# Another written-out order for a state-space layer and an MLP on one core: copies on other engines, other PSUM banks, no fillers

## The chip, the core and the metric

The kernel runs on one core of one Trainium2 chip. The metric is the device time of one execution in microseconds. The kernel before took 228.49, 229.55 and 230.34 us in three runs; the median is 229.55 us. The profile was taken in an execution of its own, in which the span from the first to the last instruction was 226.4 us. What lies outside the span (the start and end of the program) is in the time and not in the profile; the median stands 3.15 us above the span.

Engines are named as the profile names them. PE is TensorE, which multiplies matrices and writes into PSUM; DVE is VectorE; ACT is ScalarE; POOL is GpSimd; SP is SyncE, which here only issues DMAs. Each engine works through its own queue strictly in order; engines wait for each other by semaphores.

## The reference

The input is 2048 positions of 512 channels in bf16. The first half is a layer norm, followed by a convolution along the positions with a kernel made from 128 complex states per channel, and the second half is a layer norm (in effect two, merged) followed by an MLP of width 1376 with a tanh GELU:

```
x = A_u
n = layernorm(x)
K[d,l] = Re( sum_n C[d,n] * exp(dt*A[d,n] * l) * dt*B[d,n] )     # 512 x 2048, 128 states
y = irfft( rfft(n padded) * rfft(K padded) )[:2048] + n * Dskip
h = x + y
z = layernorm(layernorm(h))
out = h + ( gelu(z @ w1 + b1) @ w2 + b2 )
```

## The kernel before

The work is cut along the channels into four chunks of 128 (CW, NCH) and along the positions into two batches of 1024. The kernel K is built from tables of powers: magnitudes by exponentials on ScalarE (L793, 16 of them; L991, 10 of them) and phases by sines. A chain of products on VectorE (L1036 and L1043 in `chain`, L1068 in `chain1`) multiplies magnitudes by the sines that ScalarE makes (L1026 and L1063) from phases that TensorE accumulates (L1013, L1018, L1058, L1061). The products give the pairs of tables EA, EB, IA, IB, and TensorE multiplies them into K (`kgen`, L1092).

For `chain1` the phases must be laid out anew. They are computed on VectorE in `phase` (an arctangent on ScalarE, L883, then a run of six VectorE operations that ends in `split`, L760 to L762), written to DRAM as `HL_d` (L889) and read back (L892). The arctangent needs a product on VectorE (L877) and the table of ScalarE's functions that holds it; the eight sines of the first `chain` are queued behind it on ScalarE.

K then goes through transforms that are matrix products too (`kspec`, `kspec1`, `ktail`, `klate`, `fstage`), partly by a trip through DRAM that changes the layout. The normalised input is transformed in `austage` (L946) and `xspec` (L967, and L971 on VectorE for the second batch). In `inverse` VectorE multiplies spectra (L1235, or L1210 with sums in L1225 for the last chunk of the second batch), TensorE transforms back (L1245), a copy brings the result to SBUF, and a DMA transpose (L1261) turns it. `tail` adds the residual (L1315, L1319, L1322), makes statistics (L1323) and the second layer norm (L1334, L1336). `mlp` does the first product (L1362), the GELU on ScalarE (L1364), the second product (L1378), the sum with the residual on VectorE (L1380) and the output DMAs. There are four MLP passes of 512 positions. From the second half on, products of the MLP of the first batch are mixed with the inverse transform of the second.

Most products end in a copy from PSUM to SBUF by `evac`, which can run on ScalarE (L616) or VectorE (L618). PSUM has eight banks; an `evac` of 1024 columns frees two of them.

What sets the order of the work is a list written out in the source. The program first records 914 operations with their data dependencies (`add`). `ORDER` (L292 to L330) then lists them: an entry is twice the number of the operation, plus one if the second of its two possible engines is to run it. A negative entry is a filler: four small products of an identity on TensorE into a bank that is free and whose result nobody reads (`fill`, L1449, its products at L1451). `SLOTS` (L331) gives the PSUM bank for each new PSUM tile in the order in which they appear. `run` only reads the two strings, and the operations are emitted in the order of the list, so that the list fixes the order within each engine's queue:

```
            o = ops[k // 2]
            o.e = o.eng[k % 2]
            ...
            for p in o.new:
                p.slot = int(next(given))
```

Two fills of zeros (`gap` at L756, called at L757 and L758 for VectorE) are operations 27 and 28, entries 54 and 56 of the list. The product L877 is operation 93 (entry 186), the arctangent operation 126 (entry 252).

Of the kernel before, what the change touches and what calls it, by code (L numbers as in the profile page):

```python
# [275 lines left out]
class VS(V):  # L276
# [13 lines left out]
LAG = {"PE": 0.12, "ACT": 0.20, "DVE": 0.14, "POOL": 0.15, "SP": 0.15}  # L290
OWN = {"PE": 0.0, "ACT": 0.17, "DVE": 0.11, "POOL": 0.1, "SP": 0.0}
ORDER = [  # L292
# [35 lines left out]
]  # L328
SLOTS = "0124624620462046042642640426420206464620242002606204206242604026462064202064026406246024602406206420642016240364710404160364160743104523712460453347247364163210657000423751452706341725310671620547"


TURN = 450000
# [2 lines left out]
class Sched:  # L335
# [54 lines left out]
    def run(self, nslots):  # L390
# [13 lines left out]
        taken = [None] * nslots  # L404
        given = iter(SLOTS)
        order, seen = [], set()
# [1094 lines left out]
```

## Time and profile before

| | before |
|---|---|
| median time of three runs | 229.55 us (228.49 to 230.34) |
| span of the profiled execution | 226.4 us |
| PE busy | 198.1 us (87%) |
| DVE busy | 174.3 us (77%) |
| ACT busy | 164.9 us (73%) |
| POOL busy | 13.8 us (6%) |
| chain that ended last, by engine | PE 65%, ACT 17%, DVE 11%, DMA 3% |

A row of the chain or the timeline reads: start in us from the span's beginning, duration in us, engine, what is written, line of the kernel, number of instructions. In the timeline, square brackets give the idle time ahead and who ended it. A row of the groups reads: line, engine, operation, what is written from what, partitions x elements and types, number of instructions; then busy us in all and the mean ns of one; then the idle time just before them. In PE rows a tile such as 128\*32 is the part of the array that a product uses (rows \* columns). The slices of the page are 5.66 us each, and a digit is the busy share in tenths. "ps" is PSUM, "ar" the one large SBUF tile.

### The profile page before, as it was taken

To read this page: it belongs to the slowest core of one execution; us is meant where nothing else is said; L and a number is where in the kernel's file an instruction comes from. 1 tells how busy PE (TensorE), PEld (TensorE's weight loads), DVE (VectorE), ACT (ScalarE), POOL (GpSimd) and SP (SyncE) were. 2 spreads that over 40 slices of the span, in tenths; PEclk is the share of its full clock that TensorE was granted. 3 is DMA by queue.
4 is the path that set the end of the run, shared out by engine and by line. 5 is a ranking of instruction groups with operands and counts; after the bars stand their busy time and mean duration, and the time that the engine had idled before them with its cause. 6 is when DMAs were issued, how large, how long until landed. Compare 5 with 4: busy or idle time off the path is not lost.

```text
span 226.4 us, 6876 instructions
## 1 busy us (share of the span) xinstructions
PE 198.1 (87%) x2989; PEld 112.4 (50%) x2989; DVE 174.3 (77%) x277; ACT 164.9 (73%) x205; POOL 13.8 (6%) x26
## 2 busy tenths in 40 slices
PE   6314977768999999999999868999999999999993
PEld 3102743234767478566576556644443444444552
DVE  7999789999998898889999999899827476013022
ACT  4999999999988998989999469695156206801900
POOL 2000301200010003000000010300000101000000
PEclk9999999999999999999999999999999999999998
DMA  5992074250003964657789495383050131313202
GB/s 152 179 189 74 7 243 128 50 146 6 6 3 75 130 174 135 163 143 213 163 176 280 136 306 110 108 191 90 0 127 0 32 88 46 72 44 78 75 23 70
DMA packets 43159, 25.09 MB, mean 111 GB/s; under 512 B 30197, under 2 KB 40697, under 8 KB 43130
## 3 DMA queue, kind: packets, MB, share of 16 engines
q1 hardware_dynamic: 42968, 24.59, 45.2%
q8 instruction: 23, 0.38, 0.7%
q10 hardware_dynamic: 162, 0.07, 0.1%
q14 instruction: 6, 0.05, 0.1%
HBM read 14.13 MB, written 5.28 MB: 86 GB/s over the span
## 4 chain that ended last, share of the span: by engine, by line
PE 65%; ACT 17%; DVE 11%; DMA 3%; issue 2%; POOL 0%; DVEq 0%; ACTq 0%; SPq 0%; POOLq 0%
PE ps L1378 17%; PE ps L1362 17%; PE ps L1092 8%; ACT ar L793 7%; PE ps L1245 6%; PE ps L946 4%; DVE ar L1235 4%; ACT ar L616 4%; PE ps L967 3%; ACT ar L1063 3%; ACT ar L991 3%; DVE ar L618 2%; DMA HL_d<-ar 2%; PE ps L1145 1%; PE ps L1061 1%
## 5 line engine op out<-in xcount | busy, mean ns | idle before, releaser
L616 ACT CAST ar<-ps 128x1024 bf16<-128x1024 f32 (+4 forms) x72 | 61.9, 903 | 14.0 <-PE ps L1245 9.2
L1364 ACT ACTIVATE ar<-ps,ar 128x512 bf16<-128x512 f32 (+1 forms) x44 | 27.0, 692 | 28.7 <-PE ps L1362 20.5
L1378 PE MATMUL ps<-ar 128*128 128x512 bf16 (+3 forms) x187 | 40.2, 367 | 0.0
L1362 PE MATMUL ps<-ar 128*128 128x512 bf16 (+1 forms) x176 | 39.8, 379 | 0.0
L1380 DVE TENSOR_TENSOR ar<-ps,ar 128x512 bf16<-128x512 f32 (+1 forms) x17 | 10.8, 655 | 28.3 <-PE ps L1378 28.3
L1378 PEld LDWEIGHTS <-ar 128*128 128x128 bf16 (+1 forms) x187 | 17.9, 98 | 19.7 <-issue 0.7
L1362 PEld LDWEIGHTS <-ar 128*128 128x128 bf16 (+1 forms) x176 | 17.3, 100 | 20.5 <-issue 0.8
L1235 DVE TENSOR_TENSOR ar<-ar 128x2048 bf16<-128x2048 bf16 x20 | 23.9, 1220 | 1.0 <-PE ps L1245 0.5
L1245 PE MATMUL ps<-ar 64*128 64x128 bf16 x672 | 21.7, 216 | 3.1 <-DVE ar L1235 2.1
L618 DVE CAST ar<-ps 128x1024 bf16<-128x1024 f32 (+3 forms) x19 | 21.3, 1129 | 3.3 <-PE ps L946 1.7
L1245 PEld LDWEIGHTS <-ar 64*128 64x128 bf16 x672 | 19.0, 94 | 7.8 <-DVE ar L1235 4.6
L1063 ACT ACTIVATE ar<-ps 128x1024 bf16<-128x1024 int16 x20 | 19.7, 1027 | 1.7 <-PE ps L1061 1.0
L1092 PE MATMUL ps<-ar 128*52 128x66 bf16 x512 | 19.4, 242 | 0.3 <-DVE ar L618 0.2
L1092 PEld LDWEIGHTS <-ar 128*52 128x52 bf16 x512 | 16.9, 130 | 4.4 <-issue 2.6
L689 POOL TENSOR_TENSOR ar<-ar 128x4 f32<-128x4 f32 (+1 forms) x6 | 8.6, 1436 | 141.7 <-DVE ar L694 99.5
L946 PE MATMUL ps<-ar 128*32 128x512 bf16 x256 | 15.9, 381 | 0.5 <-ACT ar L991 0.3
L793 ACT ACTIVATE ar<-ar 128x1024 bf16<-128x1024 f32 x16 | 15.7, 1045 | 0.6 <-DVE ar L788 0.6
L1026 ACT ACTIVATE ar<-ps 128x1024 bf16<-128x1024 int16 x16 | 15.7, 1033 | 0.3 <-PE ps L1018 0.2
L1068 DVE TENSOR_TENSOR ar<-ar 128x1024 bf16<-128x1024 bf16 x20 | 13.1, 685 | 1.2 <-ACT ar L1063 1.0
L967 PE MATMUL ps<-ar 128*64 128x512 bf16 (+2 forms) x160 | 14.0, 298 | 0.1
L1322 DVE TENSOR_TENSOR ar<-ps,ar 128x512 bf16<-128x512 f32 x12 | 8.0, 683 | 7.9 <-ACT ar L1364 4.3
L1061 PE MATMUL ps<-ar 128*32 128x256 f16 (+1 forms) x256 | 12.7, 301 | 1.2 <-ACT ar L1063 1.1
(85 smaller groups left out, 232.0 us busy)
## 6 DMA issues: line engine op xcount, KB each, us to landing
ar<-in_A_u_dram SPq DMA_DIRECT2D x16, 128.0 KB
ar<-in_A_u_dram SPq DMA_DIRECT2D x8, 256.0 KB
out_dram<-ar SPq DMA_DIRECT2D x30, 64.0 KB
ar<-in_B_w_dram SPq DMA_DIRECT2D x4, 344.0 KB
ar<-in_B_w_dram SPq DMA_DIRECT2D x2, 640.0 KB
AK_d<-ar SPq DMA_DIRECT2D x2, 512.0 KB
ar<-AK_d SPq DMA_DIRECT2D x2, 512.0 KB
AKc_d<-ar SPq DMA_DIRECT2D x4, 256.0 KB
```

What stands on the lines that cost most here:

```text
L616: act.copy(out_fn(), in_fn())
L618: dve.tensor_copy(out_fn(), in_fn())
L793: add("ACT", c_act(1024) + 0.03, lambda e, e0=e0: act.activation(free(EB0 // 2 + 4 * (16 - e0), [[8 * e0, 2], [4 * NB, NCH * CW // 4], [1, ...
L946: pe.matmul(pst(p)[32 * j:32 * j + 32, 512 * z:512 * z + 512], lhsT=BX.ap()[:, f0 + z, 16 - 16 * c:48 - 16 * c], rhs=src[2 * j + c].ap(), ...
L967: pe.matmul(pst(p)[64 * h:64 * h + 64, w * (k + r):w * (k + r) + w], lhsT=T.ap()[:, f, r, :], rhs=v[f:f + 1].ap()[:, 0, :], start=True, st ...
L1063: add("ACT", c_act(1024), lambda e, sc=sc: act.activation(sc.ap().rearrange("p z a b -> p (z a b)").rearrange("p (x a f) -> p a x f", a=4, ...
L1092: pe.matmul(o, lhsT=free(ta.lo // 2 + q * 4 * NP_ + f, [[4, NP_ + NA]]), rhs=free(tb.lo // 2 + q * 4 * NB + f, [[4, 2 * NB]]), start=ta is ...
L1235: dve.tensor_tensor(pq.ap().rearrange("p n d -> p (n d)"), a, b_, ALU.mult)
L1245: pe.matmul(pst(p)[:, 512 * h + 128 * k:512 * h + 128 * k + 128], lhsT=q.ap()[rows, x, :], rhs=TP[w].ap()[rows, f0 // 2 + k, :], start=(n ...
L1362: pe.matmul(pst(p)[:fs], lhsT=w1s[dc].ap()[:, fc * P:fc * P + fs], rhs=ybuf.ap().rearrange("p (t c) k -> p c t k", c=4)[:, dc], start=(dc ...
L1364: add("ACT", c_act(512, 1), lambda e, p=p, fc=fc, fs=fs: act.activation(hT.ap()[:fs, fc, :], pst(p)[:fs], ACT.Gelu_apprx_tanh, bias=b1_sb. ...
L1378: pe.matmul(pst(p)[:, c0:c1], lhsT=hT.ap()[:fs, fc, 128 * t:128 * t + 128], rhs=w2s[fc].ap()[:fs, c0:c1], start=(fc == 0), stop=(fc == NFC ...
```

## The change

`ORDER` and `SLOTS` are replaced. The 914 operations, their data and their dependencies stay the same; what each engine does when, and some choices of engine, are different:

- The two fillers (entries -1 and -5) are gone.
- ScalarE's queue has 198 entries where it had 208, VectorE's 291 where it had 277, SP's 127 where it had 131. TensorE's 278 and POOL's 20 are only reordered. Of the operations that may run on either engine, 23 go from ScalarE to VectorE and 9 from VectorE to ScalarE; four DMA issues go from SP's queue to ScalarE's.
- Up to the last sum of spectra (L1225), VectorE has 20 operations more from ScalarE: ten copies of 1024 float columns (among them the two of 1024 columns at L843 and in the first half of `S3`, L867, and the ones of `austage` and `fstage`), one of 924, one of 264, four of 512, one of 576 on 64 partitions, one bf16 copy of 1024 and one of 512 columns, and one scaling of 512 columns out of PSUM (L1334). It has eight fewer: four copies of 1024, one of 512, a bf16 copy of 1024, and two scalings of 512.
- The two fills of zeros (entries 54 and 56), second and third in VectorE's queue before, stand between the layer norm's statistics and behind its scalings.
- On TensorE products with the same part of the array stand next to each other more often: along its queue the part changes 97 times where it changed 119 times. The products of `tail` for the second batch (L1319) stand in one group of eight.
- Two pieces of the second MLP product (L1378, six matrix products) stand ahead of the last group of L1245, and one piece of the first (L1362, four) behind it, where they stood the other way round.
- SP's queue takes the first loads in another order: slices of the input come ahead of some of the parameters, the order of the two halves of the phase tables is turned, and the constants of W come before those of T.
- PSUM tiles go to other banks.

The diff, cut to the first lines of the two lists, the lines with the entries named above, and the strings of banks:

```diff
 ORDER = [
-    294, 0, 50, 2, 4, 62, 52, 154, 6, 64, 54, 8, 102, 12, 56, 66, 14, 10, 136, 16, 68, 58, 104, 32, 190, 106, 30, 96, 98, 76, 164, 60, 26, 22, 138,
...
-    184, 430, 434, 170, 432, 436, 112, 242, 116, 438, 42, 248, 188, 130, 442, 132, 458, 448, 232, 226, 452, 454, 450, 194, 210, 244, 214, 228, 218,
-    212, 128, 202, 134, 222, 220, 196, 224, 456, 446, 216, 444, 238, 186, 240, 234, 236, 472, 475, 468, 250, 252, 284, 484, 488, 471, 487, 298, 254,
-    256, -1, 490, 302, 258, 260, 262, 300, 312, 264, 306, 304, 204, 316, 460, 314, 320, 318, 326, 328, 330, 266, 340, 310, 332, 462, 476, 342, 334,
-    280, 268, 206, 308, -5, 270, 344, 338, 346, 776, 778, 348, 792, 794, 336, 272, 286, 352, 354, 356, 324, 384, 350, 360, 358, 479, 386, 390, 274,
...
+    0, 6, 2, 4, 8, 52, 64, 50, 102, 194, 62, 12, 10, 66, 68, 154, 96, 84, 26, 86, 16, 104, 58, 72, 76, 14, 136, 106, 22, 98, 108, 78, 202, 60,
+    141, 138, 118, 120, 142, 122, 80, 144, 146, 148, 124, 151, 190, 70, 18, 32, 94, 30, 34, 152, 156, 74, 192, 28, 110, 112, 164, 176, 178, 158,
+    160, 166, 20, 162, 24, 414, 422, 168, 416, 171, 180, 172, 175, 418, 426, 126, 92, 128, 428, 424, 36, 82, 420, 204, 88, 434, 210, 100, 182,
+    430, 284, 212, 432, 226, 436, 206, 228, 242, 438, 208, 44, 40, 54, 116, 440, 218, 442, 446, 244, 458, 114, 456, 222, 454, 450, 452, 220, 448,
+    444, 56, 214, 288, 46, 224, 188, 238, 230, 240, 216, 38, 132, 246, 232, 234, 248, 236, 130, 476, 90, 472, 479, 460, 475, 468, 184, 488, 290,
+    298, 250, 463, 186, 302, 471, 491, 196, 772, 252, 300, 312, 304, 254, 314, 134, 256, 764, 306, 282, 258, 260, 316, 308, 326, 262, 318, 264,
...
 ]
-SLOTS = "0124624620462046042642640426420206464620242002606204206242604026462064202064026406246024602406206420642016240364710404160364160743104523712460453347247364163210657000423751452706341725310671620547"
+SLOTS = "1071346036024602640264024606206462002466242662060260246422064206420642426046024602462046204602462042604236013563701341437047362475270173103564261507610452173052365432601267465024572161254203721432"
```

60 rows, old and new, of the table ORDER are left out of this document.

## The prediction

> **What bounds the kernel now.** I read the page first (busy shares, the 40 slices, the chain), then the chain in order of time, then the busy time by stretch.
>
> ```profile
> span 226.4 us, 6876 instructions
> PE 198.1 (87%) x2989; PEld 112.4 (50%) x2989; DVE 174.3 (77%) x277; ACT 164.9 (73%) x205; POOL 13.8 (6%) x26
> ...
> PE   6314977768999999999999868999999999999993
> ...
> DVE  7999789999998898889999999899827476013022
> ...
> PE 65%; ACT 17%; DVE 11%; DMA 3%; issue 2%; POOL 0%; DVEq 0%; ACTq 0%; SPq 0%; POOLq 0%
> ```
>
> TensorE is the longest row, but from slice 1 to slice 28 (some 160 us) VectorE stands at 8 or 9 nearly throughout; only behind that has it room. So a copy put on VectorE is cheap late and dear early. The chain in order of time:
>
> ```profile
> 36.04 0.70 DVE ar L694
> ...
> 39.89 4.31 DMA HL_d<-ar
> 44.27 2.24 DMA ar<-HL_d
> ...
> 46.55 0.40 PE ps L1058 x4
> 46.95 0.22 PE ps L1061 x8
> ...
> 47.66 1.75 ACT ar L1063 x2
> ...
> 56.89 1.47 PE ps L1092 x40
> ...
> 163.43 0.55 PE ps L1245 x16
> 163.98 1.41 PE ps L1378 x6
> ...
> 222.89 0.04 issue
> ```
>
> A VectorE run ends in the split of the phases (L762), which goes out to DRAM and back (HL_d, 39.89 to 46.51), releases the sines of chain1 (L1063, from 47.66), and these release the first kernel products (L1092, 56.89). From there TensorE leads. The last product of the second inverse (L1245) starts at 163.43 and ends at 163.98; behind it TensorE runs to 222.89 without a wait in the chain, and 3.5 us of output follow. The busy time by stretch, cut where VectorE starts, where the split ends, at the first L1092, at 140.3, and where VectorE has finished the last combination (L1225) that the last L1245 group needs:
>
> ```profile
> core 0: us, PE busy (x) PEld busy (x) DVE busy (x) ACT busy (x) POOL busy (x), PEclk, DMA share, GB/s
> 4.42:39.88 35.46, 20.29 (x348) 12.08 (x345) 32.89 (x63) 34.83 (x40) 2.99 (x4) 1.00 0.61 138
> 39.88:56.89 17.01, 13.25 (x256) 5.69 (x249) 16.68 (x22) 16.40 (x18) 1.47 (x6) 1.00 0.24 67
> 56.89:140.30 83.41, 79.04 (x1909) 54.57 (x1909) 78.13 (x118) 73.58 (x89) 3.91 (x4) 1.00 0.61 146
> 140.30:162.40 22.10, 22.10 (x175) 11.10 (x171) 20.75 (x27) 14.06 (x20) 2.00 (x1) 1.00 0.47 115
> ```
>
> VectorE is busy 32.89 + 16.68 + 78.13 + 20.75 = 148.45 us of these 157.97: it idles 9.5 us (2.57, 0.33, 5.28, 1.35). TensorE idles 4.4 us from 56.89 to 140.3 and none after. Both engines are nearly full here, VectorE 94%.
>
> **The copies, which carry the sum.** Up to that last L1225 the new VectorE queue holds 20 operations that ScalarE had, and gives 8 away (counted by reading both orders). Their durations:
>
> ```profile
> L618 DVE CAST ar<-ps 128x1024 bf16<-128x1024 f32 x14 | 16.9, 1218 | 2.0 <-PE ps L946 1.7 <-PE ps L1120 0.3
> L1036 DVE TENSOR_TENSOR ar<-ar 128x1024 bf16<-128x1024 bf16 x16 | 10.5, 683 | 0.0
> L931 DVE TENSOR_SCALAR ar<-ar 128x512 bf16<-128x512 bf16 x16 | 5.5, 406 | 0.1
> L618 DVE CAST ar<-ps 128x512 bf16<-128x512 f32 x3 | 2.1, 692 | 0.8 <-PE ps L1145 0.6 <-ACT ar L616 0.3
> L618 DVE CAST ar<-ps 128x924 bf16<-128x924 f32 x1 | 1.1, 1120 | 0.5 <-PE ps L1092 0.5
> L618 DVE COPY ar<-ps 128x1024 bf16<-128x1024 bf16 x1 | 0.7, 676 | 0.0
> ```
>
> Added: ten copies of 1024 at 1.218 (12.2), one of 924 (1.1), four of 512 (2.8), one bf16 copy (0.7), and four small ones with no VectorE row of their own (264, 576 and twice 512 columns), between 0.4 and 0.7 each by the L931 and 512 rows, together 1.6 to 2.8; I take 2.2, the middle. Sum 19.0. Given away: four of 1024 (4.9), one of 512 (0.7), the bf16 copy (0.7), two scalings at 0.41 (0.8): 7.1. Net 11.9 us. Back to back they overlap a little:
>
> ```profile
> 1.25 1.34 DVE L756 MEMSET ar<- 128x1536 f32 x1 [0.27 <-issue]
> 2.85 1.34 DVE L756 MEMSET ar<- 128x1536 f32 x1 [0.27 <-issue]
> 4.42 0.69 DVE L689 TENSOR_TENSOR ar<-ps,ar 128x512 f32<-128x512 f32 x1 [0.23 <-ACT ar L701]
> ...
> 31.13 0.68 DVE L689 TENSOR_TENSOR ar<-ar 128x512 f32<-128x512 f32 x1
> 32.53 3.49 DVE L618 CAST ar<-ps 128x1024 bf16<-128x1024 f32 x3 [0.72 <-PE ps L946]
> ...
> 161.72 0.69 DVE L1225 TENSOR_TENSOR ar<-ar 128x512 bf16<-128x512 f32 x1
> ```
>
> Three copies take 3.49, 1.163 each, 0.955 of the mean; so 11.9 becomes 11.4. The two L756 fills of zeros ran before 4.42, while VectorE had nothing else. The change queues them among the statistics of the layer norm, behind real work: 2.6 us more. VectorE's work from 4.42 to the last L1225 becomes 148.45 + 11.4 + 2.6 = 162.45 us. With no idle at all it ends at 166.9; with the old 9.5 us of idle at 176.4; it ended at 162.4.
>
> **Where idle remains.** Through the split L762 the new queue has four more 1024 copies (4.65), two L1036 products (1.3) and the two fills (2.6) ahead of it; of the old idle of 2.57 I let 1.0 stay (the POOL power function is still waited for). The split then ends at 39.87 + 8.55 - 1.57 = 46.9, 7.0 late. The DRAM trip of 6.6 us is unchanged, so L1058 comes at 53.5, the first sine L1063 at 54.7 and L1092 at 63.9. Between 46.9 and the end of the first sine VectorE has eight products of the first chain and one copy queued, and I let it wait 1.0 us. For the rest (old idle 6.96) I take 2.5: more work queues up and ScalarE, lighter by the same copies, delivers earlier. Idle 4.5 in all, last L1225 at 171.4, last L1245 group (0.55, and a release) done at 172.1.
>
> **ScalarE's front.** Two copies of 1024 columns leave it ahead of the table load that the sines need.
>
> ```profile
> L616 ACT CAST ar<-ps 128x1024 bf16<-128x1024 f32 x47 | 46.0, 1022 | 13.1 <-PE ps L1245 9.2 <-PE ps L967 1.2 <-issue 1.1
> ```
>
> ```profile
> 35.37 0.63 ACT L701 ACTIVATE ar<-ar 128x512 f32<-128x512 f32 x1
> 36.80 3.77 ACT L1026 ACTIVATE ar<-ps 128x1024 bf16<-128x1024 int16 x4
> ```
>
> The arctangent (L883) at 35.37 could come 2.0 us earlier, at 33.4, but it waits for the product at L877 (31.13 to 31.81 before). That stands behind five more copies (5.8) and the fills (2.6), less about 1.1 of absorbed idle: done at 39.1. All eight chain sines (L1026) are queued behind the arctangent on ScalarE, so they start near 39.9 in place of 36.80. The relief is worth nothing.
>
> **TensorE.** Shape changes along its queue fall from 119 to 97 (counted on both orders). Their price:
>
> ```profile
> 60.51 0.41 PE L1018 MATMUL ps<-ar 64*32 64x512 f16 x8
> 60.85 0.69 PE L1092 MATMUL ps<-ar 128*52 128x66 bf16 x16
> ```
>
> Eight L1018 products between groups of another shape hold TensorE 0.34 us from start to start; eight L1061 after a group of the same shape take 0.22 (the chain at 46.95; both are one pass of 512 columns' time). An excursion is 0.12, a change 0.06: 22 changes save 1.3 us, of which 10 lie between L1092 and the last L1245 (0.6) and 8 behind it (0.5). The two fillers (four small products each) stand where TensorE waits anyway for ScalarE or for HL_d: nothing. Between the first L1092 and the last L1245 the work is the same but for six L1378 products drawn ahead (1.4, as the chain shows for just these at 163.98) and four L1362 of the same shape put off (0.9). TensorE alone would reach that group's end at 63.9 + 102.7 (79.04 + 22.10, and all of the 1.58 us to 163.98) + 1.4 - 0.9 - 0.6 = 166.5, with the old idle of 4.4 at 170.9. VectorE's 172.1 decides, narrowly. Behind it: 58.9 - 1.4 + 0.9 - 0.5 = 57.9 us to 230.0, plus 3.5: span 233.5. The eight L1319 groups, now in one piece, wait for a ScalarE copy and a DMA transpose behind the last L1245; 24 L1362 products cover these in the new order, where 30 products did before and nothing waited. The six missing bound the loss: 0 to 1.4 us; I take 0.
>
> **Edits at nothing.** Other PSUM banks: a bad choice costs a wait for one copy (1.2); I see none and keep it in the range. Four DMA issues go from SP's to ScalarE's queue, which has become lighter; SP's reordered loads move data that VectorE uses later than before.
>
> The span grows by 7.1 us. The median of 229.55 stands 3.15 us above this profile's span; with the same distance the time is 236.6.
>
> **The rivals.**
>
> *TensorE leads and ScalarE's front shortens (faster).* If the L877 product is there when the table is (33.4), the front is 2.0 us earlier, and the shape changes give 1.3: 226.3 us. For it: TensorE's 65% of the chain, ScalarE's 17%. Against it: VectorE's 9.5 us of idle can't hold 13.9 us of new work. It decides only if VectorE's product at L877 ends by 33.4. 6%.
>
> *The lag is made up (no change).* The split is late, but TensorE's 4.4 us of idle and VectorE's 9.5 go to nearly zero and the six early L1378 products fill in: 229.5 to 231.8. Even zero idle gives 232.1, so it needs copies cheaper than their rows. 12%.
>
> *TensorE at half pace.* A longer wait for HL_d empties TensorE. After the waits early on:
>
> ```profile
> 12.95 0.40 PE L865 MATMUL ps<-ar 128*32 128x256 f16 x1 [5.09 <-DMA ar<-tab_I]
> ...
> 22.57 2.75 PE L988 MATMUL ps<-ar 128*32 128x256 f16 x48 [2.03 <-DVE ar L618]
> 24.66 2.85 PE L988 MATMUL ps<-ar 128*32 128x256 f16 x56
> ```
>
> From 22.57 to 24.66, 40 products, 10 passes of 256 columns four abreast, take 2.09 us, about twice the pace of the L1061 row, though the granted clock reads 1.00 in every stretch above. If L1092 begins so after some 4 us without products, 6 us at half pace lose 3: TensorE's 170.9 becomes 173.9, past VectorE, span 235.3 and 238.4 us; a second such stretch gives 241.4. [...] Against it: the products of chain1 follow the sines, two in 1.75 us at 47.66, which half pace still keeps up with, and VectorE leaves TensorE 1.2 us in hand. 10%.
>
> *VectorE decides, as summed.* 72%, at 236.6.
>
> **How the numbers follow.** VectorE's idle from 0 to 9.5 spans 232.1 to 241.6; leaving out the last microsecond, and taking in the upper half of the no-change case, the range is 230.8 to 240.6. About 6% faster, 6% at the lower no-change end and 7% above are left out. Within 1% (227.3 to 231.8; about what a measurement can tell from no change): 12%. Faster 6%, slower 82%.
>
> **What would show it.** VectorE's slices at 9 through slice 29; TensorE with more idle from 40 to 64 us and again short waits on VectorE before L1245; L883 released by VectorE, not by the table load; HL_d's write starting near 47, the first L1092 near 64, the last L1225 near 171; L1319 in one group. I am wrong if the first L1092 is before 60, or if TensorE runs from it to the last L1245 without waiting on VectorE.

## The result, and the profile after

The changed kernel takes 239.98 us (median of six runs, 239.15 to 240.34) where the kernel before takes 228.95: the ratio is 1.0472, with a 95% interval from 1.0439 to 1.0505. It is slower, and the time lies inside the forecast range (230.8 to 240.6), 3.4 us above the forecast of 236.6 and close to its upper end. The profiled execution took 240.18 us with a span of 238.4 us, so 1.8 us lie outside the span. The forecast had added 3.15 us, the distance of the old median from the old profile's span; that hid a part of the miss, since in spans it is 238.4 against 233.5, 4.9 us.

Line numbers of the changed kernel are one higher than those of the kernel before (L1092 is now L1093, L1245 is L1246, L1225 is L1226). The page of the changed kernel, busy shares, slices and chain:

```profile
span 238.4 us, 6848 instructions
PE 200.7 (84%) x2973; PEld 115.6 (48%) x2981; DVE 184.4 (77%) x291; ACT 156.6 (66%) x191; POOL 14.4 (6%) x26
...
PE   6204958559899989999998885999999999999994
...
DVE  2999999995999899899999898799993748313022
...
PEclk9999988956999999999999997999999999999999
...
PE 47%; DVE 22%; issue 20%; DMA 3%; ACT 2%; POOL 2%; SPq 0%; DVEq 0%; POOLq 0%; ACTq 0%
```

ScalarE has lost 8 us of work (164.9 to 156.6) and VectorE has gained 10 (174.3 to 184.4). VectorE stands at 9 in most slices up to slice 29, TensorE has fallen to 5 in the eighth and ninth slice (42 to 54 us), and its share of the chain went from 65% to 47%, VectorE's from 11% to 22%. Of the 20% called "issue", 42.86 us are one stretch (99.98 to 142.84) in which the chain follows POOL; the timeline says that POOL waits there for VectorE (42.90 us, until L695), so VectorE's share is larger than the 22% show. The chain of the changed kernel in order of time:

```profile
46.78 4.27 DMA HL_d<-ar
...
51.10 2.20 DMA ar<-HL_d
...
53.34 0.62 PE ps L1059 x4
...
65.72 1.96 PE ps L1093 x54
...
142.88 1.93 POOL ar L690
144.83 0.17 DVE ar L695
...
145.86 0.40 PE ps L1347 x4
146.26 3.23 PE ps L1246 x64
...
153.94 1.89 PE ps L1246 x64
...
176.75 0.58 PE ps L1246 x16
177.36 5.34 PE ps L1363 x24
182.70 1.85 PE ps L1320 x16
```

HL_d's write starts at 46.78 in place of 39.89, the first kernel product comes at 65.72 in place of 56.89 (8.8 us late), the last inverse product at 176.75 in place of 163.43 (13.3 late). L1320 (the former L1319) runs in one piece and waits for nothing.

The end of the chain has another shape than the forecast gave it. TensorE's last wait of more than 0.2 us lies at L1347, at 145.86, and is 2.88 us long: VectorE's statistics end near 142.8, then come POOL's power function, VectorE's L695 and ScalarE's L1337. Behind it TensorE runs to 234.84. In the kernel before, its last such wait (0.69 us, for VectorE's L1235) ended at 138.41, and TensorE ran from there to 222.89. So of the span's 12.0 us, 7.45 lie ahead of TensorE's last wait and some 4.5 behind it, where the new list leaves TensorE more to do; 1.3 of these are half pace, 64 products of L1246 that take 3.23 us at 146.26 (granted clock 0.55 from there to 149.5) and 1.89 at 153.94 (1.00).

The busy time by stretch, with the cuts of the forecast: the end of the split, the first L1093, the first L1363, the end of the last L1226:

```profile
core 0: us, PE busy (x) PEld busy (x) DVE busy (x) ACT busy (x) POOL busy (x), PEclk, DMA share, GB/s
4.42:46.76 42.34, 22.80 (x376) 12.46 (x374) 40.65 (x70) 34.78 (x39) 3.18 (x7) 0.96 0.44 112
46.76:65.72 18.96, 13.82 (x212) 5.72 (x211) 16.07 (x21) 13.89 (x16) 1.03 (x3) 0.73 0.24 70
65.72:151.19 85.47, 77.86 (x1842) 55.21 (x1845) 79.33 (x120) 67.35 (x79) 4.97 (x5) 0.98 0.63 150
151.19:176.70 25.51, 25.30 (x240) 13.28 (x241) 24.64 (x32) 15.19 (x22) 1.86 (x1) 1.00 0.31 73
sum 172.28, PE 139.78 PEld 86.67 DVE 160.68 ACT 131.22 POOL 11.04; mean PE 34.94 PEld 21.67 DVE 40.17 ACT 32.80 POOL 2.76
```

Up to the end of the last L1226 VectorE is busy 160.68 of 172.28 us and idles 11.6 (1.69, 2.89, 6.14 and 0.87 by stretch). Before, it was busy 148.46 of 157.99 and idled 9.5. So of the 14.3 us by which this point is later, 12.2 are work and 2.1 are idle. The forecast had counted on more work (162.45) and on far less idle (4.5). Up to the first L1093 the 8.8 us are 7.1 of work and 1.7 of idle, behind it the 5.5 are 5.1 and 0.4. From the end of the last L1226 to the end of the span the changed kernel needs 61.7 us where 64.0 were needed before; the forecast had 62.1.

### The profile page after: what moved, and what is told of

It is laid out like the page before. It is cut to its first block, busy times and chain, and to the rows that moved or that the text cites. A ratio compares the mean times of both kernels' runs of the same rounds, so it can differ in the third digit from the quotient of the medians.

```text
span 238.4 us, 6848 instructions
## 1 busy us (share of the span) xinstructions
PE 200.7 (84%) x2973; PEld 115.6 (48%) x2981; DVE 184.4 (77%) x291; ACT 156.6 (66%) x191; POOL 14.4 (6%) x26
## 4 chain that ended last, share of the span: by engine, by line
PE 47%; DVE 22%; issue 20%; DMA 3%; ACT 2%; POOL 2%; SPq 0%; DVEq 0%; POOLq 0%; ACTq 0%
PE ps L1363 16%; PE ps L1379 16%; DVE ar L619 6%; DVE ar L924 4%; PE ps L1246 3%; PE ps L1093 3%; DVE ar L690 3%; DVE ar L1069 3%; DVE ar L695 2%; POOL ar L690 2%; PE ps L1062 2%; DMA HL_d<-ar 2%; PE ps L947 2%; PE ps L1059 1%; ACT ar L1064 1%
## 5 line engine op out<-in xcount | busy, mean ns | idle before, releaser
L617 ACT CAST ar<-ps 128x1024 bf16<-128x1024 f32 (+4 forms) x60 | 52.4, 920 | 21.5 <-PE ps L1246 6.2
L1365 ACT ACTIVATE ar<-ps,ar 128x512 bf16<-128x512 f32 (+1 forms) x44 | 28.0, 686 | 28.1 <-PE ps L1363 26.2
L1363 PE MATMUL ps<-ar 128*128 128x512 bf16 (+1 forms) x176 | 40.1, 379 | 0.1
L1379 PE MATMUL ps<-ar 128*128 128x512 bf16 (+3 forms) x181 | 38.7, 366 | 0.4 <-issue 0.2
L619 DVE CAST ar<-ps 128x1024 bf16<-128x1024 f32 (+5 forms) x31 | 32.6, 1066 | 2.3 <-PE ps L1146 0.8
L1363 PEld LDWEIGHTS <-ar 128*128 128x128 bf16 (+1 forms) x176 | 17.3, 100 | 20.3 <-issue 0.6
L1246 PE MATMUL ps<-ar 64*128 64x128 bf16 x672 | 22.6, 224 | 0.6 <-DVE ar L1236 0.6
L1064 ACT ACTIVATE ar<-ps 128x1024 bf16<-128x1024 int16 x20 | 19.7, 1032 | 4.2 <-PE ps L1062 3.4
L1246 PEld LDWEIGHTS <-ar 64*128 64x128 bf16 x672 | 20.1, 98 | 4.4 <-issue 1.9
L947 PE MATMUL ps<-ar 128*32 128x512 bf16 x256 | 18.3, 427 | 3.4 <-DVE ar L932 2.6
L1093 PE MATMUL ps<-ar 128*52 128x66 bf16 x512 | 18.3, 243 | 0.6 <-DVE ar L1069 0.6
L1093 PEld LDWEIGHTS <-ar 128*52 128x52 bf16 x512 | 16.7, 129 | 3.1 <-issue 1.7
L968 PE MATMUL ps<-ar 128*64 128x512 bf16 (+2 forms) x160 | 14.4, 304 | 4.1 <-DVE ar L619 1.7
L1062 PE MATMUL ps<-ar 128*32 128x256 f16 (+1 forms) x256 | 13.9, 327 | 1.5 <-ACT ar L1064 1.4
L947 PEld LDWEIGHTS <-ar 128*32 128x32 bf16 x256 | 7.4, 105 | 12.2 <-issue 5.2
```

The lines of the kernel that those rows point to most:

```text
L617: act.copy(out_fn(), in_fn())
L619: dve.tensor_copy(out_fn(), in_fn())
L947: pe.matmul(pst(p)[32 * j:32 * j + 32, 512 * z:512 * z + 512], lhsT=BX.ap()[:, f0 + z, 16 - 16 * c:48 - 16 * c], rhs=src[2 * j + c].ap(), ...
L1064: add("ACT", c_act(1024), lambda e, sc=sc: act.activation(sc.ap().rearrange("p z a b -> p (z a b)").rearrange("p (x a f) -> p a x f", a=4, ...
L1093: pe.matmul(o, lhsT=free(ta.lo // 2 + q * 4 * NP_ + f, [[4, NP_ + NA]]), rhs=free(tb.lo // 2 + q * 4 * NB + f, [[4, 2 * NB]]), start=ta is ...
L1246: pe.matmul(pst(p)[:, 512 * h + 128 * k:512 * h + 128 * k + 128], lhsT=q.ap()[rows, x, :], rhs=TP[w].ap()[rows, f0 // 2 + k, :], start=(n ...
```

## The experiments

### All 32 engine choices, in either order

In the new list the 32 operations that changed between ScalarE and VectorE were given back their old engines (a_engines_before), and in the old list they got the new ones (b_engines_after). Nothing else was edited; an entry's last bit is the engine:

```diff
 ORDER (new list)
-  ..., 141, ..., 171, ..., 463, ..., 491, ...   # operations 70, 85, 231, 245 and 28 more
+  ..., 140, ..., 170, ..., 462, ..., 490, ...
```

> The new order and banks, but all 32 copies and scalings on the engine that the old order gave them. If VectorE's load is the cause: 11.4 us of VectorE work go, VectorE no longer decides the last L1246, and most of the loss returns: 230 to 233 us. If the order and the banks themselves are the cause: 237 us or more, since only engine choices change. If TensorE's half pace is the cause: the wait for HL_d and the slow products behind it stay, so 236 us or more.

> The mirror image: the old order, banks and fillers, with the 32 engine choices of the new one. If VectorE's load is the cause: 11.4 us more on VectorE against 9.5 us of its idle, which can't all be used: 233 to 238 us. If order and banks are the cause: 228 to 231 us.

The new list with the old engines took 249.96 us (1.0892, 1.0839 to 1.0945), 10 us more than with its own engines; the old list with the new engines took 262.81 us (1.1443, 1.138 to 1.1505). The load theory fell in both. The first time lies in the open ranges of the two other theories (237 or more, 236 or more), but in the mirror image the theory of order and banks, with 228 to 231, fell as well. VectorE's work alone does not explain the times: in the first it is busy 150.88 us up to the end of the last L1226, nearly as little as in the kernel before, and idles 30.9. Neither the engines nor the order accounts for the times by itself: what an engine choice is worth depends on the place in the queue. The next two runs show that for three of the 32 operations.

### Two single choices that hold up a queue

```diff
 ORDER (new list, a_first_back)         ORDER (old list, b_two_over)
-  141                                  -  1081   1086
+  140                                  +  1080   1087
```

> The new list with one copy given back to ScalarE, operation 70 (1024 columns, the first table of phases). Theory 'VectorE has no slack, and only the load counts': 1.2 us less, 238.8. Rival 'a copy on the other engine holds up the queue it joins': on ScalarE it stands behind three exponentials at L794 and VectorE's first L848 waits for it, as where all old engines were put into the new order (L848 at 13.27 in place of 9.48, 3.8 us late); with VectorE without slack these 3.8 us go through to the end: 243 to 244.

> The old list with two operations of the second half given to VectorE in their places, as in the new list: 540 (a scaling of 512 columns in the first tail, L1334) and 543 (a copy of 512 columns of the transposed rows). Load theory: 0.4 + 0.7 us more on VectorE, 229.5 to 230.4. Rival 'held up queue': the two stand in VectorE's queue ahead of products of spectra (L1235) that the inverse transform waits for, and they themselves wait for the statistics and the power function on POOL; where all new engines were put into the old order VectorE waited 3.37 and 4.20 us near there: 4 to 7 us, so 233 to 236.

a_first_back took 243.83 us (1.0658, 1.061 to 1.0706), 3.85 us more than the changed kernel, though VectorE has a copy less. Its ScalarE and its VectorE near the place, from the timeline (start, duration, then in brackets the idle time ahead):

```profile
7.52 4.82 ACT L794 ACTIVATE ar<-ar 128x1024 bf16<-128x1024 f32 x5
12.25 0.99 ACT L617 CAST ar<-ps 128x1024 bf16<-128x1024 f32 x1
```

```profile
13.27 1.23 DVE L848 TENSOR_TENSOR ar<-ps,ar 128x1024 f32<-128x1024 f32 x1 [4.72 <-ACT ar L617]
```

The copy stands behind a row of exponentials on ScalarE (the last five are shown), and L848 starts at 13.27 where the changed kernel starts it at 9.48. The 3.8 us arrive undiminished at the end of the last L1226 (180.25 against 176.70, and 3.85 in the time). That is the held-up queue, as expected (243 to 244). The load theory, which gave 238.8, is out for this operation.

b_two_over took 238.19 us (1.0395, 1.0336 to 1.0454): 9.1 us for 1.2 us more of work on VectorE, more than the 4 to 7 expected. VectorE of that kernel, from the timeline:

```profile
138.82 0.80 DVE L1334 TENSOR_SCALAR ar<-ps,ar 128x512 bf16<-128x512 f32 x1
...
145.57 2.36 DVE L1235 TENSOR_TENSOR ar<-ar 128x2048 bf16<-128x2048 bf16 x2 [3.96 <-PE ps L1245]
...
155.80 1.22 DVE L1210 TENSOR_TENSOR ar<-ar 128x1024 f32<-128x1024 bf16 x1 [5.04 <-PE ps L1245]
```

and its TensorE:

```profile
139.68 0.61 PE L1346 MATMUL ps<-ar 128*128 128x128 bf16 x4 [3.11 <-DVE ar L1334]
...
142.36 3.60 PE L1245 MATMUL ps<-ar 64*128 64x128 bf16 x64 [0.33 <-ACT ar L616]
```

The scaling L1334 waits its turn in VectorE's queue; TensorE's L1346 waits 3.11 us for it, L1245 stands behind that in TensorE's queue, and keeps VectorE waiting in turn. What is more than expected is TensorE's pace: the granted clock is 0.88 from 140 to 180 (1.00 in the kernel before), the 64 products at 142.36 take 3.60 us (1.96 at 153.79 in the same run), and 16 products of L1362 at 148.56 take 5.30 (3.63 in the kernel before), together 3.3 us. In both whole lists these bits are set the right way for their own order. That a held-up operation holds all that stands behind it is seen where all old engines stand in the new list, with the same 4.72 us before L848: the fill L1280, which reads nothing, starts there at 19.83 in place of 16.03.

### Six copies that only shift load

Six copies for which the receiving queue has room in both orders: in the new list they go back to ScalarE (a_six_back), in the old list to VectorE (b_six_over).

```diff
 ORDER (new list, a_six_back)           ORDER (old list, b_six_over)
-  171 463 585 731 771 935              -  170 462 584 730 770 934
+  170 462 584 730 770 934              +  171 463 585 731 771 935
```

> The new list, six of the copies that went to VectorE given back to ScalarE in their places (operations 85, 231, 365 and 385 with 1024 columns, 292 with 924, 467 with 512). Theory 'VectorE has no slack in the new order': these six take 4 x 1.22 + 1.12 + 0.69 = 6.7 us on VectorE, and ScalarE idles enough to take them, so the time falls by 5 to 6.7 us, to 233.3 to 235; the split ends near 44.3 (two copies less), the last L1226 near 170. Rival 'the order of the list sets the time, and VectorE's load is not what decides': 239 to 240.5.

> The old list with the same six copies given to VectorE that a_six_back gives back (85, 231, 292, 365, 385, 467). Theory 'VectorE decides in the old order too, though it idles 9.5 us up to the last L1225': 4 to 6.7 us more, 233 to 236. Rival 'TensorE leads in the old order and VectorE's idle takes the copies in': 229 to 230.5.

b_six_over took 234.28 us, 5.2 more than the kernel before (1.0251, 1.0174 to 1.0328: clearly slower, though not clearly by more than 2%) and inside the 4 to 6.7 expected. a_six_back took 237.02 us (1.0345, 1.0288 to 1.0401), 3.0 less than the changed kernel; that is 2 us above the one expectation and 2 us below the other. Its runs scatter from 235.72 to 237.93; the profiled one, with 235.72 the quickest, has a span 4.5 us shorter (233.9 against 238.4), and the profiles are compared here. The busy time from 4.42 to the end of the last combination in each (columns as above), first b_six_over:

```profile
4.42:168.60 164.18, 136.70 (x2671) 85.23 (x2673) 154.40 (x233) 134.34 (x159) 10.38 (x15) 0.98 0.52 126
```

and a_six_back:

```profile
4.42:172.30 167.88, 136.15 (x2670) 86.44 (x2671) 155.11 (x234) 135.69 (x159) 11.05 (x16) 0.96 0.50 124
```

| | VectorE work to the last L1225 | its idle | ends at |
|---|---|---|---|
| before | 148.46 | 9.5 | 162.4 |
| before, six copies on VectorE | 154.40 | 9.8 | 168.6 |
| after, six copies back on ScalarE | 155.11 | 12.8 | 172.3 |
| after | 160.68 | 11.6 | 176.7 |

Two things follow. The six copies, 6.7 us by their rows (four at 1.22, 1.12 and 0.69), change VectorE's work by 5.94 and 5.57 us, 0.89 and 0.83 of the rows. In part that is because an operation starts before the one ahead of it has ended (in the changed kernel a copy of 1.21 us at 22.06 is followed at 23.18); the rest is not explained. And in the old order the 5.94 us of work move the end by 6.2: the 9.5 us of idle took in nothing. In the new order 5.57 us of work move it by 4.4 in the quickest run and the time by 3.0 in the median. Four of the waits show why. VectorE's timeline in the kernel before:

```profile
28.32 0.17 DVE L694 SCALAR_TENSOR_TENSOR ar<-ar 128x8 f32<-128x8 f32 x1 [1.20 <-POOL ar L689]
...
89.40 0.17 DVE L694 SCALAR_TENSOR_TENSOR ar<-ar 128x8 f32<-128x8 f32 x1 [0.54 <-POOL ar L689]
...
123.32 2.36 DVE L1235 TENSOR_TENSOR ar<-ar 128x2048 bf16<-128x2048 bf16 x2 [0.45 <-PE ps L1245]
...
145.66 0.16 DVE L694 SCALAR_TENSOR_TENSOR ar<-ar 128x4 f32<-128x4 f32 x1 [0.90 <-POOL ar L689]
```

and with the six copies added (b_six_over):

```profile
29.42 0.17 DVE L694 SCALAR_TENSOR_TENSOR ar<-ar 128x8 f32<-128x8 f32 x1 [1.20 <-POOL ar L689]
...
92.16 0.17 DVE L694 SCALAR_TENSOR_TENSOR ar<-ar 128x8 f32<-128x8 f32 x1 [0.54 <-POOL ar L689]
...
128.07 2.36 DVE L1235 TENSOR_TENSOR ar<-ar 128x2048 bf16<-128x2048 bf16 x2 [0.45 <-PE ps L1245]
...
151.73 0.16 DVE L694 SCALAR_TENSOR_TENSOR ar<-ar 128x4 f32<-128x4 f32 x1 [0.90 <-POOL ar L689]
```

The same waits, to the hundredth, 1 to 6 us later. They are round trips: VectorE gives work to another engine and then needs its answer. When VectorE comes later, the answer comes as much later. These four are 3.1 of the 9.5 us. Most of the others stay within 0.1 us as well, but not all: two waits for L1063's sines (0.22 and 0.77) are gone, so is one of 0.25, one for L1145 grew from 0.21 to 0.81, and one of 1.23 came before an L1235, while TensorE's granted clock had fallen (0.97 from 140 to 180, 1.00 in the kernel before). That the sum hardly changed is in part chance.

### Front and rest

The first 250 entries of one list (they end about where the first L1092 starts), then the remaining operations in the order of the other; PSUM banks had to be handed out anew, and the fillers are kept only with the old front.

```diff
 ORDER (h_old_front)                    ORDER (h_new_front)
+  entries 1 to 250 of the old list     +  entries 1 to 250 of the new list
+  then the new list without these      +  then the old list without these
```

> The first 250 entries of the old list (they run up to about the first L1092, with their engines, and without four of the 1024 copies on VectorE), then the other operations in the new order with the new engines; PSUM banks handed out anew. Theory 'VectorE's extra work adds up and its waits stay, so a lag is carried through to the end': the new kernel's first L1093 was 8.8 us late, so 7 to 9 us of the 11 go: 231 to 233; first L1093 near 57, last L1226 near 168. Rival 'the lag of the front is made up behind it, where TensorE and VectorE had waits to give': 237 to 240. Rival 'the front is all of it': 228 to 230.

> The mirror of it: the first 250 entries of the new list with their engines, then the other operations in the old order with the old engines; PSUM banks handed out anew, no fillers. Theory 'carried through': 7 to 9 us over the kernel before, 236 to 238. Rival 'made up behind the front': 229 to 232. Sum of this excess and of h_old_front's: about 11 us if the parts add up.

h_old_front took 232.7 us (1.0159, 1.0124 to 1.0193: less than 2%, but clearly slower), where 231 to 233 was expected, h_new_front 238.83 us (1.0439, 1.0389 to 1.0488), somewhat above the 236 to 238 expected: 3.35 and 9.5 us over the kernel before, 12.8 together where the whole change costs 11.0. Nothing was made up behind the front:

| | first L1092 | end of last L1225 | rest of the span |
|---|---|---|---|
| before | 56.9 | 162.4 | 64.0 |
| old front, new rest | 57.5 | 168.6 | 62.4 |
| new front, old rest | 66.5 | 172.4 | 64.8 |
| after | 65.7 | 176.7 | 61.7 |

The new front alone is 9.6 us late at the first kernel product and 10.0 us late at the last combination. The new middle part adds 5.5 us (0.6 to 6.2 late with the old front, 8.8 to 14.3 in the whole change), and the new end gives about 2 us back. So the span's 12.0 us are 8.8 of the front, 5.5 of the middle and 2.3 the other way from the end. Up to the last combination VectorE works 154.11 us and idles 10.1 with the old front, and works 154.99 and idles 13.0 with the new one (148.46 and 9.5 before): again no idle is used up, and the new front adds some.

### The fills of zeros

```diff
 ORDER (new list, a_zeros_first)
-  0, 6, 2, 4, 8, ... 40, 54, 116, ... 444, 56, 214, ...
+  0, 6, 2, 54, 56, 4, 8, ... 40, 116, ... 444, 214, ...
```

> The new kernel with the two fills of zeros back at the head of VectorE's queue, where VectorE has nothing else. VectorE's load: 2.6 us less work, of which up to the old idle may be lost again: 237.3 to 238.5 us, the write of HL_d about 2 us earlier than 46.78. The other theories: no change of more than 0.5 us.

It took 239.77 us (1.0449, 1.04 to 1.0497): no change, where 237.3 to 238.5 was expected from the load. Where the fills stood in the changed kernel, from VectorE's timeline:

```profile
28.93 1.34 DVE L757 MEMSET ar<- 128x1536 f32 x1 [0.27 <-issue]
...
30.50 0.17 DVE L695 SCALAR_TENSOR_TENSOR ar<-ar 128x8 f32<-128x8 f32 x1 [0.21 <-POOL ar L690]
...
33.64 1.34 DVE L757 MEMSET ar<- 128x1536 f32 x1 [0.27 <-issue]
```

and without them (a_zeros_first):

```profile
30.50 0.17 DVE L695 SCALAR_TENSOR_TENSOR ar<-ar 128x8 f32<-128x8 f32 x1 [1.75 <-POOL ar L690]
...
35.45 1.23 DVE L619 CAST ar<-ps 128x1024 bf16<-128x1024 f32 x1 [1.74 <-PE ps L947]
```

L695 starts at 30.50 in both. The fills lay inside two round trips, to POOL's power function and to the product L947; the one place where VectorE's idle is good for something is work put into the wait itself.

### Fillers against half pace

In the stretch ahead of the first L1093 the granted clock is 0.73, and the products of chain1 come at half the old pace. Six fillers ahead of entry 776 (an L968 product) and five ahead of entry 354 (the first L1059) were added to the new list.

```diff
 ORDER (new list, a_fillers)
-  332, 344, 342, 776, ... 336, 286, 352, 338, 354, ...
+  332, 344, 342, -1, -2, -1, -2, -1, -2, 776, ... 338, -1, -2, -3, -4, -1, 354, ...
```

> The new kernel with eleven fillers on TensorE: six while it waits for the last sines of the first chain and five while it waits for HL_d. If TensorE's half pace is a large part of the loss: the clock in the stretch from 47 to 66 us goes from 0.73 to near 1.0, the L1059 and L1062 groups take 0.22 in place of 0.43 us, and the time falls by 3 us or more. If VectorE's load decides: the products are faster, but the time falls by 1.7 us at most, the lag of the first L1093 that my sum did not have.

It took 240.17 us (1.0486, 1.0433 to 1.054): no gain. TensorE of the changed kernel, from the timeline:

```profile
33.43 6.19 PE L947 MATMUL ps<-ar 128*32 128x512 bf16 x80 [2.65 <-DVE ar L932]
...
47.01 0.41 PE L1019 MATMUL ps<-ar 64*32 64x512 f16 x8 [0.51 <-ACT ar L1027]
49.07 1.06 PE L968 MATMUL ps<-ar 128*64 128x512 bf16 x4 [1.66 <-ACT ar L1027]
...
53.34 0.62 PE L1059 MATMUL ps<-ar 65*32 65x512 f16 x4 [1.38 <-DMA ar<-HL_d]
53.75 0.64 PE L1062 MATMUL ps<-ar 128*32 128x256 f16 x8
54.17 0.64 PE L1059 MATMUL ps<-ar 65*32 65x512 f16 x4
```

and with the fillers (L1452):

```profile
49.29 2.72 PE L1452 MATMUL ps<-ar 128*128 128x128 bf16 x24 [1.44 <-ACT ar L1027]
...
55.55 0.40 PE L1059 MATMUL ps<-ar 65*32 65x512 f16 x4
55.78 0.39 PE L1062 MATMUL ps<-ar 128*32 128x256 f16 x8
56.00 0.39 PE L1059 MATMUL ps<-ar 65*32 65x512 f16 x4
```

From group to group chain1 steps 0.42 us in the changed kernel and 0.22 with the fillers, as in the kernel before. But the fillers and what stands behind them start chain1 2.2 us later, and the first L1093 comes at 66.30 in place of 65.72. The half pace is real, and in this stretch it costs the changed kernel some 1.6 us (53.34 to 65.72 against 55.55 to 66.30); fillers in these places pay that price themselves. Behind 66.30 the granted clock is 1.00 up to the last L1226 in this run, so the half pace at 146.26 is gone too, and the time is still the same; L1347, which starts that stretch, comes at 147.22 in place of 145.86. The slow L947 at 33.43 is as slow here (6.12 us). No run takes the half pace away without paying for it, so its full share of the 11 us stays open.

### Two further lists

> A third list: the old one with entries shifted among each other and 33 engine choices changed so that VectorE has 281 entries in place of 277 but about 1.6 us less of it lies ahead of the last L1225, and ScalarE 204; no fillers. If VectorE's work and its fixed waits up to the last L1225 set the time, then this list, in which these end 1.6 us earlier by the rows of the old trace and the rest 1 us sooner, takes 226 to 228; if half pace of TensorE or the missing fillers matter more, 229 or above.

> A list of the same kind as n_moved (the old one with entries shifted by short steps and 28 engine choices changed, no fillers, banks handed out anew), but with the 131 entries of SP's queue in exactly the old order, where n_moved had nearly all of them in other places and VectorE waited 7.20 us for a late load and TensorE 5.62 us for HL_d. Theory 'n_moved failed by its DMA order': no such wait is left; VectorE's copies up to the last L1225 are about as many as in the old kernel, and its waits are 1 to 2 us fewer, so 226 to 229. Rival 'shuffled engine queues lose by themselves': above 235.

```diff
 ORDER (n_moved, n_moved_dma)
-  the old list with its two fillers
+  its 914 operations, most of them shifted by short steps, with 34 (n_moved) or 28 (n_moved_dma) engine choices changed
```

Both failed. n_moved took 268.59 us (1.1742, 1.1681 to 1.1804). VectorE's timeline:

```profile
96.76 0.69 DVE L924 BATCH_NORM_STATS2 ar<-ar 128x6 f32<-128x512 bf16 x1 [7.20 <-DMA ar<-in_B_b_dram]
```

SP issued the last six pieces of the input only from 85.68 to 89.45, behind other transfers, and the statistics of the second batch waited for them (the row names in_B_b, which SP issued next, at 89.49). n_moved_dma is another list of the kind, with SP's queue in the old order. This wait is gone and the time is 23 us lower, though the other engines' queues differ as well and how much SP's order gave is not shown. But 245.55 us (1.0743, 1.0712 to 1.0774) is still far above the 226 to 229 expected:

```profile
4.42:174.88 170.46, 136.68 (x2668) 83.26 (x2666) 147.98 (x228) 139.52 (x162) 10.22 (x13) 0.94 0.50 121
```

VectorE's work up to the last L1226 is 147.98 us, as in the kernel before, and its idle 22.5 where 8 had been expected. Which of the shifted entries make these waits was not pursued. No version that beats both kernels came out.

## Why the prediction was right, and where it was wrong

- **VectorE decides** (72%): right up to 146 us, not shown behind it. Moving copies alone moves the time in both orders. From the first L1093 to 142 us TensorE waits for VectorE seven times by 0.2 us or more (3.0 us in all), and its 2.88 us before L1347 go back to VectorE's statistics. But the path was not the one forecast, through the last L1225: behind 145.86 TensorE waits for nothing of more than 0.2 us, and the last L1246 starts right behind other products, 0.05 us after the last L1226 ends (1.0 after it in the kernel before). There both engines are full (25.30 and 24.64 of 25.51 us), and which of them leads the trace does not tell.
- **The split and the trip through DRAM**: forecast 46.9, 53.5, first sine 54.7; measured 46.76, 53.34, 55.30. The sum was right by luck, since its parts were not. The two fills (2.6 us) were free, but the product L947, at half pace after a wait, held up the copies behind it: 80 products took 6.19 us (granted clock 0.50 from 34.0 to 37.2) where 64 took 3.74 before.
- **ScalarE's front is worth nothing**: right. L877's product ended at 39.8 (forecast 39.1), and the chain's sines started at 40.4 (39.9).
- **The first L1092 at 63.9**: it came at 65.7. Half pace of TensorE, the 10% rival, was there, but ahead of the first L1092 (some 1.6 us) and again at 146.26 (1.3 us), not in L1092 itself. The terms of its sum, some 4 us without products and then 6 us at half pace, are shown by no run: the longest wait of TensorE between 42 us and the first L1092 was 1.66 us, and in the changed kernel the granted clock was 0.50 from 34.0 to 37.2, from 47.65 to 57.7 and from 146.6 to 149.9. The time by itself lies between that rival's two figures (238.4 and 241.4); what speaks for VectorE as the main cause are the runs with six copies and the sum of its work, 12.2 of the 14.3 us.
- **VectorE's work, 162.45 us**: measured 160.68. The overlap factor of 0.955, from three copies in a row, was too high; six copies measured 0.89 and 0.83.
- **"Idle 4.5 in all"**: this is the step that failed. Stage by stage 1.0, 1.0 and 2.5 were forecast; 1.69, 2.89 and 7.01 were measured, so that most of the miss lies behind the first L1093. Its reason, "more work queues up and ScalarE, lighter by the same copies, delivers earlier", treated idle as slack. The six copies in the old order left it at 9.8. With the old 9.5 left as they were, the prediction's own sum gave 176.4 for the last L1225; it was 176.70. That this comes so near is luck: the work was 1.8 too high and the idle 2.1 higher than before, and the new list's waits are for the most part others than the old one's (2.06 for L1064's sines, 1.44 for L1347).
- **The no-change rival** ("the lag is made up") fell for the same reason; the new front's 9.6 us were 10.0 at the last combination. **The faster rival** fell by its own condition: L877's product ended at 39.8, not by 33.4. And b_six_over shows that VectorE's work counts in the old order too, although the chain there is TensorE's by 65%.
- **Behind the last inverse, 57.9 us and 3.5**: measured 57.5 (177.33 to 234.84) and 3.5. L1320 needed no cover. The price of the shape changes was not tried alone, nor were the banks.
- **The frame outside the span** (3.15) was 1.8: the median had been set against the profile of a quicker run.

## What to carry to other kernels

An engine's idle time in a trace is slack only if the work that it waits for does not itself wait for that engine; a round trip moves along with every microsecond that is added ahead of it, as four of 0.45 to 1.20 us did here, unchanged 1 to 6 us later, so charge added work in full unless it fits into a wait by name. In kernels with written-out queues the engine of a copy and its place in the queue are one choice: a single bit cost 3.85 us here and two cost 9, of which some 3 were TensorE's half pace behind the wait. Sums over a queue's rows are good for what they hold fixed, and say little once the queues are reshuffled.

## What was not expected of the hardware

TensorE's pace fell by half without a long wait. Ahead of the slow L968 at 49.07 (four products 1.06 us, 0.62 at full pace) the longest wait was 1.66 us, behind groups of L1019 with waits of 0.51 us between them. The granted clock had already gone from 1.00 (up to 47.5) to 0.50 (from 47.65) when that wait had lasted 0.2 us; in the 4 us up to 47.5 TensorE had been busy for 2.14. The 80 L947 products at 33.43 were slow after a wait of 2.65, with 1.08 us busy in the 4 up to 33.4. In the kernel before, 2.26 us busy in 4 (42.5 to 46.5, with most of the wait of 1.35 us for HL_d in them) left the clock at 1.00. What sets the drop off is not shown. The way back is seen with the fillers: they started at 49.29 at half pace (24 products of 128 columns in 2.72 us), TensorE worked on without a gap, and the next 20 products, at 54.34, took 1.29 us. The granted clock, 0.52 from 46.76 to 53.3 and 0.98 from 53.3 to 66.3, puts the return near 53.8, about 4.5 us after the first filler (an estimate from these two means). And unlike the slow L988 products of the kernel before (from 22.57), which the prediction had found beside a granted clock of 1.00 and for which that trace has no record of the clock (its first is at 27.0 us), these show in the column: 0.73 for the stretch.
